# A kernel driven by one list of steps: the list is replaced by another order of the same steps

## The chip, the cores and the metric

The kernel runs on one core of one Trainium2 chip. The metric is the device time of one execution in microseconds, the median of several runs. Before the change it is 539.5 us, from 538.19 to 539.94 in three runs.

## The reference

The inputs are q, k and v of 4 batches, 8 heads, 576 positions and 64 channels, a random matrix omega (128 x 64), and the weights of two layers of experts. Everything is float32.

1. Attention with random features. For each head, phi(x) = exp(x omega^T - |x|^2/2 - max) / sqrt(128), with the maximum over the 128 features of one position. num = phi(q) (phi(k)^T v), den = phi(q) sum(phi(k)), and the output is num / (den + 1e-6).
2. The heads are laid side by side: 2304 tokens of 512 channels.
3. First layer of experts. Each of 8 experts has w1 (512 x 1024) and w2 (1024 x 512). A token goes to the expert with the largest logit; its output is relu(x w1) w2, times the softmax probability of that expert, times a sigmoid gate of that expert.
4. Second layer of experts: the same without the sigmoid gate.

## The kernel before, in words

**Tiling.** Attention works on 16 pairs of heads (4 batches x 4 pairs; the pair's number is one hexadecimal digit). Positions lie in two halves of 288 for q and in chunks of 128 (parts 0: three chunks, 1: two) for k. The expert layers work on 8 units, each one batch in one layer, in the order of `ORDER`; of each unit only the expert that most of its tokens chose is computed for all 576 tokens, weighted by a row of coefficients (zero for other tokens). What is left over is done for up to 8 tokens of one expert by a `Block`, and after that by a loop that seldom runs. Weights and activations of the expert matmuls are split into a high part (`wh`, `xh`, `hh`) and a remainder (`wl`, `xl`, `hl`), and each product is the sum of three matmuls (`TERMS`).

**What sets the order.** The program is emitted under `manual_schedule`: each engine (TensorE, VectorE, ScalarE, GpSimd, and SyncE, whose queue issues nearly all DMAs) executes its instructions in the order of emission, and waits by semaphores for the data and the buffers. The order is the string `PLAN`. A loop at the end of the kernel goes through its words. A number n stands for n expert steps. One expert step is 6 matmuls (line 92); the 512 steps are numbered 0 to 511 here, 64 for a unit, and 32 of these are the first product (every second one ends with an eviction on ScalarE, line 513, and one on VectorE, line 514) and 32 the second (every fourth one ends with an eviction, lines 533 and 535). Expert sums use two PSUM banks, all else the other six. A plus sign behind a copy puts it on VectorE in place of ScalarE.

**The words**, p being the pair:
- `a`, `b`, `c` load q, k and v of a pair (lines 148, 156, 164); `q`, `r` project a half of q and copy it out of PSUM; `t` is the maximum over partitions, an all-reduce on GpSimd (line 226), `s` its subtraction on VectorE (line 230), `x` the exponential on ScalarE. `k`, `m`, `e` project a part of k, take its maximum on VectorE and exponentiate on ScalarE (e: pair, part, head).
- `v`, `w` form phi(k)^T v and copy it; `n`, `d`, `f`, `g` form the numerator, divide, transpose and copy out; `h`, `l` make the high and low parts of the output, `o` stores it.
- `Gu` is the next of 11 stages of unit u's router, numbered G0.0 to G0.10: logits on TensorE, copy, transpose (.2), maximum and mask on VectorE (.3), counting matmul (.4), the expert's number (.5), coefficients (.6, .7), transpose (.8), copy, store. `Pu` reads the expert's number into SyncE; `Wu` loads the coefficients.
- `Fui`, `Hui`, `Lui` fetch tile i of unit u's weights (lines 458 and 463; two staging buffers), make its high part and its remainder (line 486). `Xuc`, `Yuc` (line 552) split the unit's output for the next layer, `Suc` stores it.
- `A` (34 stages) is the block of leftover tokens, `B` (12 stages) adds its result to rows already stored: four loads of old rows (line 757), then additions (line 766) and stores (line 768). `C` and `M` scale and merge. `J` loads the router's weights, `z` are spins of TensorE, `I` and `T` set up.

Of the kernel before, what the change touches and what calls it, by code (L numbers as in the profile page):

```python
# [63 lines left out]
Y02 G2 2 o7 t91 H17 X03+ L17 1 s90 P2 2 x90 4 F20 H20+ m80 ba o5 e801 e800 1 L20 3 Y03 F21 H21 F22 2 s91 6 ab 1 ac H22
2 L21 2 x91 G2 v80 v81 k90 k91 w8+ n80 n81 m90 e900 m91 d80 d81 e901 e910 e911 F23 1 L22 2 ca X10 1 qa0 ka0 ma0 ka1
ra01 ra00 qa1 ra11+ ta1 ma1 1 ea00 G2 1 ea11 1 G2 G2 ra10+ H23+ L23 bb F24 sa1 ea01 1 ta0 v90 v91 sa0 ea10 va0 w9 va1
wa+ S130 xa1 H24+ bc kb0 kb1 kc0 cb xa0 bd mb0 eb01 mb1 eb10 mc0 eb00 3 eb11 G3 n90 G3 ec01 d90 ec00 F25 n91 d91 vb0
vb1 wb+ qb0 rb00 qb1 kd0 rb10+ rb01 kd1 rb11+ kc1 md1 mc1 ed11 ec11 md0 1 L24 1 G3 2 ec10 1 H25+ 3 G3 1 Y10 3 L25 G2
# [5 lines left out]
1 L40 S310 1 h9+ G4 G4 H41 L41 1 F42 F43 l9 1 ha gc0 la hb 2 lb 1 H42 L42 F44 3 H43 L43 ce 8 H44+ 1 F45 1 S330 14 L44
3 F46 2 G4 fc1 gc1+ H45+ qd0 ke0 me0 qd1 rd11 rd10+ rd00+ td0 W4 S320 3 H46 rd01 1 L45 sd0 F47 td1 1 ee01 xd0 3 sd1 1
ee00 qe0 re01 re00+ qe1 kf0 re11 re10 te1 te0 oc xd1 hc+ lc kf1 ke1 me1 ee11 cf mf1 ee10 ef10 1 mf0 se1 xe1 2 ef00 1
S210 se0 ef11 1 o9 nd0 ef01 nd1 dd0 dd1 qf0 rf01 rf00 qf1 rf10 rf11+ 1 tf1 fd0 tf0 gd0 3 fd1 L46 gd1+ xe0 ve0 ve1 sf1
X40 S400 sf0 we xf1 xf0 vf0 ne0 de0 vf1 S300 ne1 wf de1 nf0 hd nf1 df0 df1 ld 1 fe0 fe1 1 H47+ ff0 ff1 ge0 ge1 he+ le
gf0 1 gf1 G5 G5 1 L47 G5 G5 1 G5 1 G5 G5 P5 1 F50 F51 G5 2 S420 2 hf lf 3 H50+ L50 2 G5 H51+ F52 1 S430 L51 1 F53 3
H52 1 Y40 1 G5 G5 2 H53+ 4 of L52 F54 8 L53 F55 9 H54+ L54 1 H55 1 W5 1 G6 X41 2 G6 3 L55 Y41 1 G6 1 X42+ Y42 G6 F56 1  # L80
H56 F57 L56 2 G6 X43 G6 P6 Y43 H57 G6 4 F60 2 L57 od 3 F61 G6 S410 4 H60 L60 H61+ 1 F62 L61 H62 1 L62 4 F63 F64 oe 3
S530 H63+ 4 L63 4 H64 L64 G6 1 F65 2 S500 5 G7 H65 G6 1 G7 G7 G7 L65 1 G7 1 G7 G6 1 F66 1 F67 W6 G7 P7 1 ob G7 T 2 A 1
H66 G7 G7 G7 2 A 2 A S510 S520 2 A 1 W7 A C50 X50 H67 C52 Y50 7 C51 L66 L67 F70 F71 1 C53 A X51 Y51 X52 Y52 3 A 2 X53+
# [891 lines left out]
```

## Time and profile before

| | before |
|---|---|
| median of 3 runs | 539.5 us |
| the profiled execution, whole | 539.03 us |
| its span, first to last instruction | 537.2 us |
| granted TensorE clock, mean | 0.998 |
| DMA | 74.18 MB, 138 GB/s in the mean |

How to read it: times are microseconds from the span's start. An engine's busy time is the union of its instructions. Matmuls overlap in the records (one of 128 x 288 is recorded with some 295 ns, and the next one starts some 133 ns later), so TensorE's pace is read from start to start. A row of the timeline gives start, duration, engine, line, operation, written and read tile, shapes, the count of merged instructions, and in brackets the idle time before it with what ended it. In the names, `qhh<-qhh,qhl` is the subtraction `s`, `PARTITION_ALL_REDUCE qhl<-qhh` the reduce `t`, `wl<-wr,wh` is `L`, `xl<-y,xh` is `Y`, `pc`, `ptc` and `pg` belong to the router, `pm` to the expert steps.

### The profile page before, as it was taken

Reading aid. Unit: us, or ns where it says so; the run is one execution under the profiler, and the core shown is the slowest. Engines: PE = TensorE matmul, PEld = TensorE weight load, DVE = VectorE, ACT = ScalarE, POOL = GpSimd, SP = SyncE. Lnnn points to the kernel's source line nnn. Section 1 sums busy time; section 2 is a strip of 40 time slices with the busy share of each in tenths; the row PEclk is TensorE's granted clock in tenths of the full one; section 3 lists DMA queues with packets and bytes.
Section 4 is the critical chain, followed back from the end, with each engine's and each line's share of the span. In section 5 each row is a group of like instructions: output and inputs, shape, how many; then the busy total and the mean of one; then the engine's idle time right before and its main releaser. Section 6 shows DMA issues by size and latency. Waiting matters only on the chain.

```text
span 537.2 us, 12915 instructions
## 1 busy us (share of the span) xinstructions
PE 525.2 (98%) x5294; PEld 503.6 (94%) x5294; DVE 341.9 (64%) x761; ACT 199.0 (37%) x503; POOL 74.0 (14%) x68
## 2 busy tenths in 40 slices
...
GB/s 307 119 56 218 120 79 177 89 120 88 206 186 153 127 86 149 103 147 177 165 0 106 192 48 98 163 3 195 70 101 146 179 114 140 188 158 89 313 169 182
DMA packets 83954, 74.18 MB, mean 138 GB/s; under 512 B 14256, under 2 KB 68144, under 8 KB 83888
## 3 DMA queue, kind: packets, MB, share of 16 engines
...
q10 hardware_dynamic: 288, 0.13, 0.1%
...
## 4 chain that ended last, share of the span: by engine, by line
PE 88%; DVE 8%; issue 2%; DMA 1%; ACT 1%; POOL 1%; POOLq 0%; DVEq 0%; ACTq 0%
PE pm L92 74%; PE pn L268 3%; PE ph L219 3%; PE ph L185 2%; DVE qhh L230 2%; DVE nm L195 2%; PE pkv L242 2%; PE pg L337 1%; PE pf L302 1%; DVE wl L486 1%; DMA wr<-w1a 1%; PE idle L850 1%; POOL qhl L226 0%; DVE wh L131 0%; DVE xl L320 0%
## 5 line engine op out<-in xcount | busy, mean ns | idle before, releaser
L92 PE MATMUL pm<-xh,wh 128*128 128x288 f32 x512 | 152.8, 298 | 1.1 <-DVE hl L514 1.1
L92 PE MATMUL pm<-hh,wh 128*128 128x288 f32 x512 | 153.4, 300 | 0.0
L92 PE MATMUL pm<-xh,wl 128*128 128x288 f32 x512 | 151.0, 295 | 0.0
L92 PE MATMUL pm<-hh,wl 128*128 128x288 f32 x512 | 150.8, 295 | 0.0
L92 PE MATMUL pm<-hl,wh 128*128 128x288 f32 x512 | 150.8, 294 | 0.0
L92 PE MATMUL pm<-xl,wh 128*128 128x288 f32 x512 | 150.8, 294 | 0.0
L514 DVE SCALAR_TENSOR_TENSOR hl<-pm,hh 128x288 fp32r<-128x288 f32 x128 | 58.3, 456 | 93.7 <-ACT hh L513 93.2
L513 ACT ACTIVATE hh<-pm 128x288 fp32r<-128x288 f32 x128 | 52.8, 412 | 156.3 <-PE pm L92 154.7
L226 POOL PARTITION_ALL_REDUCE qhl<-qhh x32 | 66.8, 2128 | 282.1 <-DVE qhh L131 144.3
L92 PEld LDWEIGHTS pm<-xh,wh 128*128 128x128 f32 x512 | 96.1, 188 | 3.1 <-DVE hl L514 1.5
L92 PEld LDWEIGHTS pm<-hh,wh 128*128 128x128 f32 x512 | 96.2, 188 | 2.5 <-issue 2.0
L92 PEld LDWEIGHTS pm<-hl,wh 128*128 128x128 f32 x512 | 96.1, 188 | 0.0
L92 PEld LDWEIGHTS pm<-xl,wh 128*128 128x128 f32 x512 | 96.1, 188 | 0.0
L92 PEld LDWEIGHTS pm<-xh,wl 128*128 128x128 f32 x512 | 96.1, 188 | 0.0
L92 PEld LDWEIGHTS pm<-hh,wl 128*128 128x128 f32 x512 | 96.0, 188 | 0.0
L486 DVE TENSOR_TENSOR wl<-wr,wh 128x1024 fp32r<-128x1024 f32 (+1 forms) x72 | 81.1, 1139 | 5.9 <-ACT wh L133 5.4
L533 DVE TENSOR_TENSOR y<-pm,cb 128x288 f32<-128x288 f32 x56 | 25.4, 454 | 40.4 <-PE pm L92 36.7
L133 ACT CAST wh<-wr 128x1024 fp32r<-128x1024 f32 (+1 forms) x36 | 35.8, 998 | 40.3 <-DMA wr<-w1b 18.7
L199 ACT ACTIVATE kp<-ph,nm 128x128 f32<-128x128 f32 x140 | 40.2, 382 | 10.1 <-DVE nm L195 10.1
L234 ACT ACTIVATE qhh<-qhh 128x576 f32<-128x576 f32 x32 | 21.9, 697 | 23.1 <-DVE qhh L230 23.0
L230 DVE TENSOR_TENSOR qhh<-qhh,qhl 128x576 f32<-128x576 f32 x32 | 30.0, 944 | 0.4 <-POOL qhl L226 0.3
L195 DVE TENSOR_REDUCE nm<-ph 128x3 f32<-128x384 f32 (+1 forms) x64 | 27.5, 481 | 3.1 <-PE ph L185 2.9
...
## 6 DMA issues: line engine op xcount, KB each, us to landing
...
qr<-qT SPq DMA_DIRECT2D x16, 288.0 KB, 4.4
kr<-kT SPq DMA_DIRECT2D x16, 288.0 KB, 3.9
xd<-xraw SPq DMA_DIRECT2D x16, 288.0 KB, 4.3
```

The lines of the kernel that those rows point to most:

```text
L92: nc.tensor.matmul(out, ws(*t), xs(*t), start=first and t == terms[0], stop=last and t == terms[-1])
L133: nc.scalar.copy(out=out, in_=in_)
L195: nc.vector.tensor_reduce(out=nm[:, j, 0:m], in_=pk, axis=AX.X, op=ALU.max, negate=True)
L199: nc.scalar.activation(self.kp[:, c, j * NF : (j + 1) * NF], self.pk[part][j][:, i * NF : (i + 1) * NF], AF.Exp, bias=self.nm[part][:, j, ...
L219: nc.tensor.matmul(ps[i], om[r, :], self.qr[r, tokens(s)], start=True, stop=True)
L226: nc.gpsimd.partition_all_reduce(qm, qe, 128, bass_isa.ReduceOp.max)
L230: nc.vector.tensor_tensor(out=qe, in0=qe, in1=qm, op=ALU.subtract)
L234: nc.scalar.activation(qe, qe, AF.Exp, scale=SCALE)
L486: nc.vector.tensor_tensor(out=wl[:, p], in0=self.raw[i][:, p], in1=wh[:, p].bitcast(F32), op=ALU.subtract)
L513: nc.scalar.activation(hh[:, s], pm, AF.Relu)
L514: nc.vector.scalar_tensor_tensor(out=hl[:, s], in0=pm, scalar=0.0, in1=hh[:, s].bitcast(F32), op0=ALU.max, op1=ALU.subtract)
L533: nc.vector.tensor_tensor(out=y[:, t], in0=pm, in1=self.cb[:, t], op=ALU.mult)
```

## The change

The string `PLAN` is replaced. Both lists hold the same steps and 512 expert steps; spins are 16 and 11 in place of 16, 8 and 3. Plus signs are 84 in place of 73 (r 13 for 17, g 15 for 8, h 10 for 8, w 6 for 5, X 8 for 5, H 32 for 30). No other line changes. Cut to the parts that matter: the opening up to the first expert steps, the passage from unit 0 to unit 1, the router of unit 3, and the end.

```diff
-a0 I z16 q00 r000+ r001 q01 b0 k00 a1 k01 r010 r011 m00 e000 b1 q10 a2 a3 r101+ z8 q11 t00 r100+ m01 c0 s00 e001 k10
-e011 b2 t01 e010 r110+ k11 b3 v00 v01 c1 c2 c3 x00 m10 r111 t11 t10 a4 s01 e100 x01 m11 w0+ q20 n00 e110 n01 r200+
-e101 q21 r201 s11 a5 e111 k20 r210 d00 d01 r211 k21 x11 v10 m20 v11 e200 s10 w1 b4 f00 b5 f01 t20 m21 g00+ g01+ x10 z3
-n10 e211 t21 q30 s20 e201 q31 e210 s21 h0+ r300 r301 r310 r311 t31 d10 k30 q40 t30 x20 x21 r401 r400 m30 n11 e301 v20
...
-x40 r501 a6 r500 d31 n40 n41 h2 e501 q51 J f30 d40 f31 r510 d41 l2 t50 g30 k51 k60 m51 r511 g31 G0 h3 b7 e510 k61 e511
-G0 G0 m60 e601 c6 e600 s50 a7 v50 m61 e610 G0 t51 G0 e611 b8 l3 f40 g40 v51 o0 k70 w5 k71 G0 x50 s51 m70 m71 q60 x51
-r600 n50 e700 n51 e710 e711 c7 v60 v61 G0 e701 v70 v71 d50 q61 r601 f41 d51 r610 P0 F00 H00+ F01 L00 f50 w7+ f51 1
...
-h6+ l6 q80 h7+ q81 a9 r800 r801 l7 r811 t81 G1 r810+ G1 1 G1 G1 1 G1 G1 t80 G1 1 b9 s80 4 s81 1 G1 x80 2 q90 q91 r901
-r900+ P1 r911 r910 x81 k80 k81 F10 H10+ F11 H11 L10 L11 F12 Y00 G2 X01 m81 1 G2 1 t90 3 F13 1 H12 3 G1 L12 F14 5 G1 G1
...
-o8 qc0 qc1 cc rc00 rc11 cd h8 l8 bf 1 rc01 H32+ L32 F34 1 ae tc1 sc1 1 rc10 2 S220 G3 1 S200 tc0 2 G3 fa0 1 ga0+ 5 fa1
...
-1 S600 1 L74 F76 2 A A 2 A A A A A 5 H75 4 H76+ 1 L75 L76 4 F77 1 A A A 5 A A H77+ 1 A A A L77 A A 3 A 8 A A B B B B B
-M700 B B B M710 S710 B B B M720 B S700 1 S720 4
+a0 I z16 q00 q01 r000+ r001+ b0 k00 k01 r011+ r010 t00 t01 m00 a1 q10 m01 a2 r101 r100+ z11 q11 s00 e001 e011 r111+
+t11 b1 a3 e010 k10 k11 e000 m10 x00 c0 v00 v01 c1 c2 c3 r110 t10 b2 s01 b3 m11 e100 q20 w0+ x01 n00 e101 n01 r200+ s11
+e110 r201 q21 e111 k20 d00 r210 t20 d01 k21 f00 m20 r211 t21 a4 x11 e200 s10 x10 v10 v11 m21 w1+ f01 g00+ e210 e201
+g01 n10 o0 s20 q30 e211 q31 s21 r300 r301 r311 t31 r310 t30 q40 h0+ k30 x20 d10 c4 r401 n11 r400 v20 v21 k31 b4 b5 m30
+e301 d11 e300 x21 q41 w2+ r410 r411 t41 t40 l0 k40 a5 f10 f11 m31 e310 e311 g10 s31 g11 m40 e400 e401 n20 n21 s30 k41
...
+e500 q50 q51 x40 r500 n40 d31 n41 h2 l2 e501 r510 t50 r501 r511 t51 d40 f30 f31 k51 g30 g31 h3 d41 b6 m51 e510 e511
+k60 J m60 G0 k61 G0 e601 G0 b7 b8 s50 x50 m61 e610 e611 e600 v50 G0 l3 G0 v51 k70 c7 w5 f40 G0 g40 s51 k71 P0 F00 F01
+v60 m70 v61 c8 m71 x51 n50 b9 e700 n51 e710 e701 e711 q60 v70 v71 r600 G0 d50 q61 d51 f50 H00+ L00 r601 w7 H01 f41
+g41+ r610+ t60 L01 f51 3 G0 2 F02 F03 2 H02 H03+ 2 L02 2 o2 1 F04 3 L03 2 H04 1 L04 4 a7 2 G0 g50+ 2 r611 t61 2 s61 1
...
+P1 l7 1 F10 5 s80 H10+ L10 s81 q90 r900 r901 q91 r910 k80 F11 r911 t91 t90 H11 L11 k81 ba F12 F13 G2 1 m81 G2 1 G1 1
+Y00 2 H12+ 2 H13+ 2 L12 1 L13 G1 X01 G1 6 F14 H14+ F15 4 H15 3 L14 F16 1 G2 G2 6 G2 S000 L15 W1 1 S030 1 m80 2 Y01 2
...
+1 ed01 2 F30 X13 ed11 g80+ H27 H30 2 Y13 L27 F31 g90 g91+ sb0 G3 5 xb0 1 f81 L30 F32 g81+ H31 na0 na1 da0 da1 nb0 nb1
+qc0 rc00 qc1 rc11 rc10 tc0 G3 1 G3 L31 db0 fa0 2 db1 F33 2 sc0 rc01 tc1 H32+ 2 fa1 kc1 1 mc1 sc1 xc1 1 L32 4 fb0 ga0+
...
+A L76 8 L77 A S610 3 A A A A B B B B B M710 M700 S710 B B B S700 B B B M720 1 B S720 4
```

## Rows read from the trace of the kernel before

**Rows 1.** The page, busy time of each engine and its share of the span.
```profile
PE 525.2 (98%) x5294; PEld 503.6 (94%) x5294; DVE 341.9 (64%) x761; ACT 199.0 (37%) x503; POOL 74.0 (14%) x68
```
**Rows 2.** The chain of waits: start, duration, instruction, count of merged ones.
```profile
54.81 24.00 PE pm L92 x180
...
445.66 64.43 PE pm L92 x486
```
**Rows 3.** Busy time by stretch: length, then each engine's time (instructions), clock, DMA.
```profile
20.00:40.00 20.00, 19.28 (x376) 16.08 (x373) 18.76 (x46) 18.89 (x61) 9.06 (x6) 1.00 0.29 84
```
**Rows 4.** TensorE's waits: who waited for whom, total, times, longest.
```profile
PE pby L734 <- ACT yc L728: 0.4, 1, 0.4
```
**Rows 5.** Timeline of VectorE and GpSimd, 11.9 to 15 us.
```profile
11.98 1.67 DVE L230 TENSOR_TENSOR qhh<-qhh,qhl 128x576 f32<-128x576 f32 x1
14.80 0.80 DVE L230 TENSOR_TENSOR qhh<-qhh,qhl 128x576 f32<-128x576 f32 x1
...
11.89 1.96 POOL L226 PARTITION_ALL_REDUCE qhl<-qhh  x1 [0.93 <-ACT qhh L133]
13.76 2.04 POOL L226 PARTITION_ALL_REDUCE qhl<-qhh  x1
```
**Rows 6.** Timeline of VectorE, GpSimd and TensorE, 42 to 45.5 us.
```profile
42.44 1.71 DVE L230 TENSOR_TENSOR qhh<-qhh,qhl 128x576 f32<-128x576 f32 x1
...
42.31 2.04 POOL L226 PARTITION_ALL_REDUCE qhl<-qhh  x1
...
45.25 0.20 PE L378 MATMUL pc<-top,unit 72*128 72x64 bf16 x1 [1.09 <-DVE top L364]
```
**Rows 7.** The same three engines, 113 to 122 us.
```profile
113.97 0.46 DVE L533 TENSOR_TENSOR y<-pm,cb 128x288 f32<-128x288 f32 x1 [0.59 <-PE pm L92]
115.69 3.37 DVE L486 TENSOR_TENSOR wl<-wr,wh 128x512 fp32r<-128x512 f32 x3
118.98 1.69 DVE L552 TENSOR_TENSOR xl<-y,xh 128x576 fp32r<-128x576 f32 x1
...
118.10 2.78 POOL L226 PARTITION_ALL_REDUCE qhl<-qhh  x1
...
121.76 0.40 PE L92 MATMUL pm<-xh,wh 128*128 128x288 f32 x1 [1.05 <-DVE hl L514]
```
**Rows 8.** The same three engines, 241 to 245.5 us.
```profile
242.00 1.70 DVE L230 TENSOR_TENSOR qhh<-qhh,qhl 128x576 f32<-128x576 f32 x1
...
241.47 2.43 POOL L226 PARTITION_ALL_REDUCE qhl<-qhh  x1
...
245.03 0.22 PE L427 MATMUL ptc<-ident,g 72*64 72x72 f32 x1 [1.05 <-DVE g L423]
```
**Rows 9.** Timeline of SyncE's issues, ScalarE and VectorE, 48 to 58 us.
```profile
48.06 1.01 SPq L458 DMA_DIRECT2D wr<-w1a  x2
...
54.26 1.05 ACT L133 CAST wh<-wr 128x1024 fp32r<-128x1024 f32 x1 [0.45 <-DMA wr<-w1a]
...
55.34 2.02 DVE L486 TENSOR_TENSOR wl<-wr,wh 128x1024 fp32r<-128x1024 f32 x1 [0.40 <-ACT wh L133]
57.28 0.45 DVE L514 SCALAR_TENSOR_TENSOR hl<-pm,hh 128x288 fp32r<-128x288 f32 x1
```
**Rows 10.** SyncE's issues, TensorE, VectorE, 17 to 30 us; the page's DMA issues.
```profile
17.08 0.92 SPq L156 DMA_DIRECT2D kr<-kT  x2
...
26.44 1.15 PE L185 MATMUL ph<-omk,kr 64*128 64x128 f32 x12
...
28.81 1.01 DVE L195 TENSOR_REDUCE nm<-ph 128x3 f32<-128x384 f32 x2
...
kr<-kT SPq DMA_DIRECT2D x16, 288.0 KB, 3.9
```
**Rows 11.** The page's DMA issues (last: median us to landing); VectorE at 522 us.
```profile
outT<-y SPq DMA_DIRECT2D x15, 288.0 KB, 4.9
...
522.28 0.82 DVE L766 SCALAR_TENSOR_TENSOR old<-by,state,old 128x576 f32<-128x576 f32 x1 [2.14 <-POOL by L745]
```

More of the change, by code (lines that the diff above doesn't have):

```diff
@@ L54 @@
-s30 d20 k50 x31 t40 m41 x30 t41 e411 d21 f20 f21 s41 m50 e410 v40 v41 h1 w3 s40 n30 x41 e500 n31 w4 l1 g20 g21 q50 d30
-x40 r501 a6 r500 d31 n40 n41 h2 e501 q51 J f30 d40 f31 r510 d41 l2 t50 g30 k51 k60 m51 r511 g31 G0 h3 b7 e510 k61 e511
-G0 G0 m60 e601 c6 e600 s50 a7 v50 m61 e610 G0 t51 G0 e611 b8 l3 f40 g40 v51 o0 k70 w5 k71 G0 x50 s51 m70 m71 q60 x51
-r600 n50 e700 n51 e710 e711 c7 v60 v61 G0 e701 v70 v71 d50 q61 r601 f41 d51 r610 P0 F00 H00+ F01 L00 f50 w7+ f51 1
-g41+ r611+ H01 L01 2 t61 F02 1 H02 1 L02 F03 1 H03+ 4 F04 1 G0 1 H04 L03 6 L04 h4+ 2 w6 3 s61 7 G0 G0 F05 g50 g51 H05+
@@ L64 @@
[L64 to L68, printed above, removed]
@@ L69 @@
-o4 6 F26 F27 be 1 tb0 2 S100 sb0 xb0 W2 H26+ X11 Y11 S110 6 X12 G3 H27+ f80 1 S120 Y12 X13 1 L26 ad tb1 f90 G3 g90
-ed10 2 P3 ed00 7 Y13 1 sb1 L27 F30 F31 H30+ L30 xb1 2 g80 1 ed01 2 f81 G3 g81 H31 na0 F32 da0 na1 nb0 da1 nb1 L31 F33
-o8 qc0 qc1 cc rc00 rc11 cd h8 l8 bf 1 rc01 H32+ L32 F34 1 ae tc1 sc1 1 rc10 2 S220 G3 1 S200 tc0 2 G3 fa0 1 ga0+ 5 fa1
-db0 db1 2 G3 H33 G3 W3 L33 1 H34+ ga1 fb0 oa fb1 f91 g91 gb0 gb1+ 2 sc0 1 xc1 xc0 G4 G4 L34 vc0 vc1 vd0 wc nc0 nc1 dc0
-dc1 vd1 3 S230 1 wd 19 af 2 F35 H35+ L35 F36 4 G4 F37 G4 2 G4 H36+ fc0 H37 1 L36 1 G4 3 L37 P4 2 G4 G4 4 F40 F41 1 H40
@@ L74 @@
[L74 to L83, printed above, removed]
@@ new lines @@
+e110 r201 q21 e111 k20 d00 r210 t20 d01 k21 f00 m20 r211 t21 a4 x11 e200 s10 x10 v10 v11 m21 w1+ f01 g00+ e210 e201
+g01 n10 o0 s20 q30 e211 q31 s21 r300 r301 r311 t31 r310 t30 q40 h0+ k30 x20 d10 c4 r401 n11 r400 v20 v21 k31 b4 b5 m30
+e301 d11 e300 x21 q41 w2+ r410 r411 t41 t40 l0 k40 a5 f10 f11 m31 e310 e311 g10 s31 g11 m40 e400 e401 n20 n21 s30 k41
+d20 v30 m41 v31 c5 k50 x31 e411 e410 d21 a6 w3 s41 f20 f21 h1 x30 m50 l1 g20 g21 v40 s40 v41 c6 x41 w4 n30 d30 n31
+e500 q50 q51 x40 r500 n40 d31 n41 h2 l2 e501 r510 t50 r501 r511 t51 d40 f30 f31 k51 g30 g31 h3 d41 b6 m51 e510 e511
@@ new lines @@
+qa0 ra00 F23 F24 ab S130 ra01 H23+ ka0 ma0 G2 ea00 ka1 bc ma1 qa1 ra10 ra11 ta1 ta0 2 ea01 1 ea11 L23 ea10 1 G2 G2 H24
+L24 G2 ac v90 va0 va1 v91 w9 wa kb0 kc0 kb1 mb0 eb00 sa1 eb01 o4 mb1 sa0 cb eb11 2 eb10 1 G3 G3 n90 mc0 ec00 n91 vb0
+Y10 vb1 ec01 bd qb0 wb d90 kd0 d91 S120 kd1 rb00 md1 rb01 S100 cc md0 qb1 rb11 tb1 rb10 tb0 1 G3 f80 2 ed10 sb1 6 W2 8
+cd 2 F25 H25 F26 o5 H26 2 o7 1 be 4 xa0 f90 ed00 G3 X11+ 2 G3 f91 L25 1 S200 xa1 L26 F27 G3 1 P3 1 xb1 2 Y11 X12+ Y12
+1 ed01 2 F30 X13 ed11 g80+ H27 H30 2 Y13 L27 F31 g90 g91+ sb0 G3 5 xb0 1 f81 L30 F32 g81+ H31 na0 na1 da0 da1 nb0 nb1
@@ new lines @@
+qc0 rc00 qc1 rc11 rc10 tc0 G3 1 G3 L31 db0 fa0 2 db1 F33 2 sc0 rc01 tc1 H32+ 2 fa1 kc1 1 mc1 sc1 xc1 1 L32 4 fb0 ga0+
+ga1+ 1 H33+ 2 ec10 ec11 ad gb0+ 1 fb1 gb1 3 G4 L33 vc0 bf G4 vd0 F34 G3 vc1 vd1 wc+ h8+ xc0 H34 L34 ob nc0 nc1 dc0 F35
+5 G3 W3 H35+ 4 L35 3 l8 S220 5 F36 1 H36 L36 3 G4 G4 F37 3 dc1 1 H37+ L37 G4 G4 2 P4 1 S230 4 F40 1 H40 1 F41 2 h9+ 7
+H41 G4 1 S310 2 L40 L41 1 F42 wd 4 l9 ha la hb lb H42+ 4 L42 1 F43 H43 1 L43 F44 F45 3 G4 4 G4 2 ae G4 af H44+ 3 H45+
+2 S330 1 L44 3 G4 F46 L45 1 W4 3 H46 3 fc0 ke0 qd0 gc0+ qd1 F47 rd10 L46 me0 1 rd00 td0 rd01 rd11 td1 S320 1 o9 1 H47
@@ new lines @@
+sd0 xd0 L47 ee00 4 sd1 2 ee01 qe0 re01+ re00 qe1 re10+ te0 re11 te1 S210 oa kf0 ke1 me1 kf1 mf1 mf0 ef10 ee11 ee10
+ef11 xd1 2 X40+ se1 2 ef01 1 fc1 gc1+ nd0 se0 oc ef00 xe0 hc+ xe1 nd1 qf0 dd0 qf1 lc rf10+ rf01 rf11 tf1 dd1 rf00 tf0
+ce 4 fd0 fd1 ve0 cf ve1 gd0 sf1 gd1+ xf1 we+ sf0 vf0 od xf0 ne0 vf1 de0 wf ne1 de1 nf0 df0 nf1 df1 1 fe0 ge0 fe1 S410
+1 ge1+ ff0 gf0 ff1 1 gf1 S300 hd+ ld he+ le G5 G5 hf+ 1 G5 lf G5 1 G5 2 G5 P5 1 G5 G5 F50 1 F51 5 G5 G5 G5 1 H50+ L50
+1 H51+ 4 L51 1 Y40 4 F52 H52+ 2 X41 1 F53 2 L52 3 F54 2 H53 1 oe 1 L53 F55 1 H54 7 W5 2 S400 L54 S420 2 G6 G6 H55+ 1
```

16 lines of the change are left out of this document (11 added, 5 removed).

## The prediction

> **What bounds the kernel now.** I read the page first. TensorE is busy for 98% of the span [rows 1], so nothing but TensorE's own waits and the opening can give time back. The chain of waits says where it is full: from 445.66 us on, 486 block matmuls follow one another in 64.43 us, 132.6 ns each [rows 2]; no order of steps makes that shorter, and both lists hold the same matmuls. The first long run of them begins at 54.81 us [rows 2]. Ahead of it stands the attention of batch 0, and there the windows show VectorE as full as TensorE (18.76 of 20 us between 20 and 40) [rows 3]. TensorE's waits of a microsecond are three after the first spin: pc in the opening [rows 6], pm at 121.76 [rows 7] and ptc at 245.03 [rows 8]. The 0.4 of pby [rows 4] is part of a matmul, copy, transpose sequence that is adjacent in both lists, so it stays.
>
> All three have one cause, which the timelines show when VectorE is laid beside GpSimd. A VectorE instruction with its operands in SBUF that starts shortly behind the start of a GpSimd all-reduce takes about 0.95 us longer. In the opening, subtraction s01 starts 0.09 us behind its reduce and takes 1.67 us; s11 starts 1.04 behind the next one and takes 0.80 [rows 5]. s50 starts 0.13 behind a reduce and takes 1.71, and pc then waits for VectorE until 45.25 [rows 6]. Y00 (0.88 behind, 1.69 us) precedes the eviction that pm waits for [rows 7]; sc1 (0.53 behind, 1.70) precedes the gate step that ptc waits for [rows 8]. I call this a collision: 0.95 us of VectorE for a start within about 1 us of a reduce's start, nothing later than that.
>
> The Trainium skill's page "SBUF — State Buffer" (section "Who interferes with whom") says that whichever of the two starts first keeps the shared ports for the whole instruction and the other blocks fully. By that, s11 could not have ended before 15.80, where its reduce ends; the trace has it end at 15.60. The measurement decides here. By the page's rule the new list's s50 would be held until its reduce ends, some 0.8 us more than I reckon below, and the sum would be 538.2.
>
> **The change part by part.** The sum is made against the profiled execution: span 537.2, 539.03 in all (1.83 around the span). The median of the runs is 539.5, so what comes out below is taken off 539.5.
>
> Opening. The steps ahead of the first expert step are nearly the same set, and TensorE's are exactly the same, 27 spins included. Two things differ in time. First, pair 1's copies: the new list has r111+ on VectorE right behind s00, in place of r111 on ScalarE behind an exponential. The reduce t11 waits for that copy. It started at 11.89 [rows 5]; r111+ would end at about 11.0 (s00's end by the trace, 10.7, plus a copy of 0.36 from start to start), so t11 starts at 11.05, and s01, which cannot start before 11.95, is 0.9 behind it instead of 0.09. It keeps 0.1 of its 0.95: s01 and what follows come 0.8 earlier. VectorE then waits for k20 at about 17, so I let 0.6 of it through. Second, q51 and r510 stand ahead of n40 in place of behind f30: t50 starts at 39.2 instead of 39.83, its successor t51 ends its first microsecond at 42.2, and s50, at about 42.4, goes free: 0.9 off the chain s50, m61, top, pc, and as much off the expert's number, which the first weight load waits for. Against that VectorE has more to do: w1+ and w2+ (about 0.2 each), six copies r of batch 0 for five (0.36), and g01 leaves it (0.28): 0.5 later. Sum of the opening: -0.6 - 0.9 + 0.5 = -1.0. Its bounds: 0, if what is late next is weight tile 1. It is issued right behind the two halves of tile 0; ScalarE's copy of it starts on its landing at 54.26, L01 ends at 57.36, and the eviction of step 1 stands behind that until 57.73, when step 4 wants its bank [rows 9]. These move with the expert's number, by 0.9 at most, and L01 has a collision of its own (2.02 us) that the new list keeps. At the other end -1.5, if both gains arrive in full.
>
> Unit 1's first matmuls (pm, 1.05). Between the last eviction of unit 0 (step 63, from 113.97 to about 114.35) and the one that step 68 waits for, the old VectorE order is r900+, H10+, L10, L11, Y00, m81; the new one s80, H10+, L10, s81, L11, m81, with Y00 behind the eviction. Two subtractions (0.74 each) in place of a copy and Y00 (0.36 + 0.67) are 0.45 more, but VectorE need not wait for q90's matmul (0.8). Added up from 114.35: s80 115.1, H10 115.8, L10 117.0, s81 117.75, L11 118.9, m81 119.55, eviction 120.0, where step 68 is due at 120.5. The slack is 0.5 and the two reduces t91 and t90 still fall into this stretch: no collision costs nothing, one 0.45, two 1.4. L10 and Y00 had one each (the 3.37 us of three L instructions hold the first, rows 7). I take 0.6, near to one: a gain of 0.45, bounds -0.35 and 1.05.
>
> Unit 2's gate (ptc, 1.05). The new list puts G3.7 behind da1 and ahead of step 183, and no reduce starts there before it: L30 1.24, g81+ 0.28, da0 0.83, da1 0.67, G3.7 0.79 make 3.8 us of VectorE against f, n and q matmuls and one step, 4.7 us of TensorE. It has 0.9 to spare, so the 1.05 goes. Bounds 0 and 1.05.
>
> What is new and could cost. Eleven more copies go to VectorE in all (84 plus signs for 73), 5.1 us of VectorE and 6.5 fewer of ScalarE; beside some 480 us of expert steps, with VectorE busy for 64% of the span [rows 1], that is hidden except where VectorE stands in a burst. I allow 0.4 for one half collision at a tight place (the gate and kp steps with under 0.4 to spare); bounds 0 and 1.5.
>
> What I cost at nothing. (a) SP's queue: o0, the store of pair 0's output, now stands ahead of c4, b4, b5, a5 and c5, and waits for g01, at about 21. b4 was issued with b5 at 17.08 and now goes at about 22. A load of this kind lands 3.9 us later; k40 ran at 26.44 and m40, its reader, started at 28.81 [rows 10]. VectorE's order covers it; without that cover, in the slowest case (c5, behind it in the same burst, took 5.6), k40 is late by 1.2 and m40 by nothing. (b) J, the gates' weights, now waits behind c6 for v41 (35.4) and is issued at about 36 instead of 31.3; landing after 3.7 us it precedes G0.0 at 41.25 by 1.5. (c) c8, b9 and a7 now stand behind F00 and F01; their readers are units later. (d) In the tail S610 now stands right ahead of the loads of old rows. If these wait until it has landed (4.9), old arrives by about 522 instead of 518, and the block's first addition starts at 522.28 behind GpSimd in any case [rows 11]; the last eviction, ten microseconds later, does not see it.
>
> Sum: -1.0 - 0.45 - 1.05 + 0.4 = -2.1. 539.5 - 2.1 = 537.4 us.
>
> **The rivals.**
> - The opening's gain is eaten by weight tile 1 and the eviction behind L01, and t91 and t90 collide twice: 0 - 1.05 + 0.35 + 0.4 = -0.3, 539.2. For it: L01's collision stays, and two reduces remain at the tight place. Against it: tile 1's issue moves with the expert's number.
> - Slower: new collisions in the stretch from 14 to 38 us, where VectorE goes from one instruction to the next and hands every delay on to the first expert step. The old list has five from s01 [rows 5] to s50 [rows 6], s01, l0, s31, s30 and s50, of 0.35 to 1.1 us. The new order of reduces (t31, t30, t41, t40) meets l0, s31, s30, s41 and s40 at other moments. Each one more costs 0.95; two more cancel the forecast's gain, and from four on the kernel is slower than can be taken for no change: 4 x 0.95 - 2.1 = +1.7, 541.2. For it: nothing in either list keeps these starts apart. Against it: of the old five, two go by the reckoning above, so that six new ones would have to come.
> - More than forecast: the opening gives 1.5, pm goes altogether, nothing new is met: -1.5 - 1.05 - 1.05 = -3.6, 535.9.
>
> **How the numbers follow.** A measurement of this kernel can tell about 0.3%, 1.6 us, from no change. Forecast (537.4; its own range 536.4 to 538.3) 0.38, first rival 0.35, slower 0.15, more 0.12. The range for 8 in 10 goes from 535.7 to 540.4. Faster, below 537.9: 0.12 and nearly all of the forecast, 0.48. Within: 0.37. Slower: 0.15.
>
> **What would show it.** Right: s01 near 0.75 us long; s50 too, with pc waiting for VectorE less than 0.4; the first long run of block matmuls at about 53.8; no ptc wait; a pm wait at step 68 of 0 to 1.4. Wrong: b4's landing behind 27.6 with m40 waiting for k40; a first expert step later than 54.8; more than five subtractions of batch 0 of over 1.05 us; a wait for weights (hl, wl) in a later unit, which no row of before shows.

## The result and the profile after

The changed kernel takes 534.22 us (median of 5 runs, 533.15 to 534.61); beside them the kernel before took 539.94 (538.19 to 541.34). The ratio is 0.9896, 95% interval [0.9867, 0.9925]: 5.6 us, 1.0% faster, where 2.1 us were forecast. Its profiled execution took 534.12, with a span of 532.3.

The page's first part and the end of the chain of waits, of the kernel after (answering [rows 1, 2]). TensorE is busy as long as before, and 4.4 of the 4.9 us that the span lost were its idle time. The experts start at 51.52, 3.0 earlier, but their first long run only at 55.45: a wait at step 4 cuts it in two. The chain in front of that wait is the landing of weight tile 1 (52.72), L01, and the eviction of step 1 behind it.

```profile
PE 524.7 (99%) x5294; PEld 503.8 (95%) x5294; DVE 341.7 (64%) x771; ACT 190.8 (36%) x493; POOL 71.7 (13%) x68
```

```profile
46.51 6.18 DMA wr<-w1a
52.72 1.06 ACT wh L133
53.84 1.11 issue
54.94 0.46 DVE hl L514
55.45 0.66 PE pm L92 x3
...
441.68 63.64 PE pm L92 x480
```

TensorE's waits of the whole kernel after: who waited for whom, total, times, longest. The 1.1 us of pc, of pm at step 68 and of ptc ([rows 6 to 8]) are gone; pby [rows 4] is there, and one pm wait is new, the one of 0.5 at step 4 in the chain above.

```profile
PE idle L850 <- POOL zeros L828: 1.1, 1, 1.1
PE pm L92 <- DVE hl L514: 0.5, 1, 0.5
PE ph L219 <- DMA qr<-qT: 0.5, 1, 0.5
PE pby L734 <- ACT yc L728: 0.4, 1, 0.4
PE pn L268 <- ACT kp L199: 0.3, 1, 0.3
```

The same view of the kernel before, from 10 to 56 us alone. Of these the prediction names only the first; the sum is 3.5 us, and after has 0.3 ahead of its first expert step in that stretch.

```profile
PE pc L378 <- DVE top L364: 1.1, 1, 1.1
PE pn L268 <- DVE kvr L131: 0.7, 1, 0.7
PE pkv L242 <- ACT kp L199: 0.5, 1, 0.5
PE pn L268 <- ACT qhh L133: 0.5, 1, 0.5
PE pf L302 <- DVE kvr L131: 0.3, 1, 0.3
PE ph L185 <- DVE qhh L131: 0.2, 1, 0.2
PE pf L302 <- ACT kp L199: 0.2, 1, 0.2
```

A subtraction that a reduce does not touch takes 0.75 us; one that takes longer is called held here. VectorE's timeline after, and GpSimd's below it: s01 and s50 (answering [rows 5, 6]), s31 and s30 between them, L10 and s81 ahead of step 68 [rows 7]. s01 starts 0.94 us behind its reduce, s50 1.01 behind t51 (the second half of the 3.91). Neither takes more than 0.83. In a second trace of the changed kernel s50 takes 0.83 again, but s01 starts 0.68 behind its reduce and takes 1.07.

```profile
11.68 0.82 DVE L230 TENSOR_TENSOR qhh<-qhh,qhl 128x576 f32<-128x576 f32 x1
...
26.45 0.75 DVE L230 TENSOR_TENSOR qhh<-qhh,qhl 128x576 f32<-128x576 f32 x1
28.05 0.77 DVE L230 TENSOR_TENSOR qhh<-qhh,qhl 128x576 f32<-128x576 f32 x1
...
40.50 0.83 DVE L230 TENSOR_TENSOR qhh<-qhh,qhl 128x576 f32<-128x576 f32 x1
...
113.30 2.23 DVE L486 TENSOR_TENSOR wl<-wr,wh 128x512 fp32r<-128x512 f32 x2
115.46 0.74 DVE L230 TENSOR_TENSOR qhh<-qhh,qhl 128x576 f32<-128x576 f32 x1
```

```profile
10.74 3.91 POOL L226 PARTITION_ALL_REDUCE qhl<-qhh  x2 [0.66 <-DVE qhh L131]
...
37.62 3.91 POOL L226 PARTITION_ALL_REDUCE qhl<-qhh  x2 [6.66 <-DVE rd L289]
...
113.72 2.09 POOL L226 PARTITION_ALL_REDUCE qhl<-qhh  x1 [7.24 <-ACT qhh L133]
```

Expert steps of all the traces, laid side by side. "Start" is the first key matmul of pair 1 (k10; 9.64 us before), which moves by up to 1 us with the first loads. The next columns are the starts of expert steps 0, 8, 72, 216 and 511 against the kernel before, each counted from k10. "End" is the time from VectorE's last instruction to the end of the span (4.16 before). The new opening does three more spins ahead of k10 and three fewer behind it; they take TensorE 0.4 us before (19.75 to 20.18), so its rows show up to 0.4 us of gain that only this way of counting makes.

```
trace               k10    step 0     8     72    216    511    end
after              +0.24   -3.28  -2.51  -3.58  -5.25  -5.00   4.00
after, again       -0.06   -2.85  -2.39  -3.37  -5.04  -4.97   4.45
new open, old rest -0.20   -2.89  -1.84  -1.85  -1.85  -1.86   5.63
  the same, again  -0.30   -2.86  -1.75  -1.75  -1.72  -1.73   5.89
old open, new rest +0.21   +0.36  +0.29  -0.73  -2.40  -2.36   4.02
old, fills         -0.15   -0.30  -0.31  -1.59  -3.09  -3.19   4.40
new, fills         +0.34   -1.55  -1.28  -2.54  -4.09  -2.82   5.33
Y00, sc1 moved     +0.11   -0.03  -0.03  -1.35  -2.55  -2.50   4.39
r111 for r110      -0.71   -0.97  -0.98  -0.97  -0.98  -0.94   3.28
  the same, again  -1.00   -1.01  -1.01  -1.01  -0.99  -0.99   5.87
pair 5's order     -0.34   -0.85  -0.86  -0.86  -0.85  -0.85   3.38
four moves         -0.30   -0.30  -0.32  -1.62  -2.80  -2.81   4.39
new, r110 back     +0.31   -1.51  -1.04  -2.10  -3.77  -3.35   4.00
l0 behind s31      -0.34   +0.03  +0.03  +0.03  +0.02  +0.02   4.38
m31 ahead of l0    -0.35   +1.35  +1.34  +1.35  +1.35  +1.36   5.92
five (l0)          +0.45   -1.17  -1.17  -2.47  -3.68  -3.64   5.52
five (m31)         -0.04   -1.15  -1.16  -2.47  -3.68  -3.69   3.34
new, L01 and A.28  +0.38   -2.88  -2.94  -2.68  -4.35  -4.63   6.11
new, A.28 alone    -0.55   -2.89  -2.03  -3.09  -4.58  -4.95   5.57
```

Of the 5.0 us at the last step, 2.5 stand at step 8 (the opening) and 1.05 more at step 72 (pm). The rest is not ptc alone. Between steps 72 and 216 the two lists also place the steps differently among TensorE's other work; taken where the same work is done, both traces of after gain 0.8 at step 136 and 0.8 more by step 203 (ptc), and lose 0.1 to 0.3 again by step 303. The place at step 136 is one that neither the prediction nor an experiment names. Before, L23 starts 0.45 us behind a reduce and takes 2.05; the copy `w` that follows it is late, and a weight load of TensorE waits 0.34 for it, which the view of the matmuls' waits does not list. After, L23 is free:

```profile
183.53 2.05 DVE L486 TENSOR_TENSOR wl<-wr,wh 128x1024 fp32r<-128x1024 f32 x1
183.08 2.23 POOL L226 PARTITION_ALL_REDUCE qhl<-qhh  x1 [0.62 <-DVE qhh L131]
187.53 0.63 PEld L185 LDWEIGHTS ph<-omk,kr 64*128 64x128 f32 x9 [0.34 <-DVE kvr L131]
...
181.70 1.23 DVE L486 TENSOR_TENSOR wl<-wr,wh 128x1024 fp32r<-128x1024 f32 x1 [0.54 <-PE pkv L242]
```

The end is as long as before.

### The profile page after: what moved, and what is told of

The parts are those of the page before. It is cut to its first block, busy times and chain, and to the rows that moved or that the text cites. A ratio compares the mean times of both kernels' runs of the same rounds, so it can differ in the third digit from the quotient of the medians.

```text
span 532.3 us, 12918 instructions
## 1 busy us (share of the span) xinstructions
PE 524.7 (99%) x5294; PEld 503.8 (95%) x5294; DVE 341.7 (64%) x771; ACT 190.8 (36%) x493; POOL 71.7 (13%) x68
## 4 chain that ended last, share of the span: by engine, by line
PE 94%; DMA 2%; DVE 1%; ACT 1%; issue 0%; SPq 0%
PE pm L92 77%; PE pn L268 4%; PE ph L219 3%; PE ph L185 3%; PE pkv L242 3%; PE pg L337 2%; PE pf L302 1%; DMA wr<-w1a 1%; DMA qr<-qT 1%; DVE nm L195 1%; PE pyc L726 0%; PE pu L705 0%; PE pt L346 0%; PE idle L850 0%; ACT wh L133 0%
## 5 line engine op out<-in xcount | busy, mean ns | idle before, releaser
L226 POOL PARTITION_ALL_REDUCE qhl<-qhh x32 | 65.1, 2075 | 278.7 <-ACT qhh L133 245.2
L486 DVE TENSOR_TENSOR wl<-wr,wh 128x1024 fp32r<-128x1024 f32 (+1 forms) x72 | 79.8, 1122 | 12.0 <-ACT wh L133 11.0
L133 ACT CAST wh<-wr 128x1024 fp32r<-128x1024 f32 (+1 forms) x35 | 34.0, 973 | 45.2 <-DMA wr<-w1b 22.8
L230 DVE TENSOR_TENSOR qhh<-qhh,qhl 128x576 f32<-128x576 f32 x32 | 27.6, 865 | 1.3 <-POOL qhl L226 1.3
```

The lines of the kernel that those rows point to most:

```text
L133: nc.scalar.copy(out=out, in_=in_)
L226: nc.gpsimd.partition_all_reduce(qm, qe, 128, bass_isa.ReduceOp.max)
L230: nc.vector.tensor_tensor(out=qe, in0=qe, in1=qm, op=ALU.subtract)
L486: nc.vector.tensor_tensor(out=wl[:, p], in0=self.raw[i][:, p], in1=wh[:, p].bitcast(F32), op=ALU.subtract)
```

## The experiments

My theory: a VectorE instruction is held by a reduce that has just started, TensorE pays where that instruction stands right ahead of what it reads, and these few places make the whole gain. The rivals: the gain is spread over the burst (VectorE has less to do ahead of a deadline), or it comes from the eleven copies that went to VectorE.

**Each half alone.** The new list's steps up to the first expert steps with the old list's rest, and the other way round.

```diff
-PLAN = old list
+PLAN = new list up to step 0 of unit 0, then the old list    # new open, old rest
+PLAN = old list up to there, then the new list               # old open, new rest
```

> The new list up to the first expert step, the old list behind it (steps that the new opening already holds are left out there, a7 is put at its start). In the trace of after, step 4 begins 2.37 us earlier than before, so if the opening's gain is handed on: 539.9 - 2.4 = 537.5 us, with the old waits of 1.05 at pm (step 68) and at ptc (G3.8) still in it. Rival, the two parts hang together (the old rest meets the earlier opening with new waits): 539 or more.

> The old list up to the first expert step, the new list behind it (c8, b9, H01, g41+, t60 and L01 are put at its start, a7 is left out there). By the traces the rest gains 4.76 - 2.37 = 2.4 us: 537.5, without waits at step 68 and G3.8. Rival, the new rest needs the new opening: 539 or more.

Old opening, new rest: 537.28 us, ratio 0.9964 [0.9949, 0.9978]; both 1.05 waits are gone. New opening, old rest: 539.06, ratio 0.9999 [0.9988, 1.001], although every expert step is 1.8 us earlier. A second trace of it:

> The new list's opening with the old rest a second time, for another trace. In the first the expert steps were 2.05 us earlier from step 8 to the last, and the span was 0.6 shorter. If the order alone sets it, the steps stand as in the first trace to within 0.3 us, counted from the first key matmul; what is lost then stands behind the last matmul (last store issued or landed 1 to 2 us later than in the kernel before) or ahead of the first.

It took 538.66 in its one run. The steps are the first trace's to within 0.13 us, and the end is 5.89 us long instead of 4.16. So in these two traces the steps are the same, and the end can take 1.5 us or more back.

**No reduce at all.** In both lists GpSimd copies 8 columns and fills the rest with zeros instead of reducing; the maximum over partitions is left out.

```diff
-            nc.gpsimd.partition_all_reduce(qm, qe, 128, bass_isa.ReduceOp.max)
+            nc.gpsimd.tensor_copy(out=qm[:, 284:292], in_=qe[:, 284:292])
+            for n in (S, S, S, HS):
+                nc.gpsimd.memset(qm[:, 0:n], 0.0)
```

> The old list, with each all-reduce on GpSimd replaced by an instruction sequence that lasts about as long, 2.0 us (a copy of 8 columns that reads both halves of q, then four fills of the result with zeros), so that nothing waits for less but GpSimd hardly reads SBUF; the maximum over partitions is left out of the computation. Theory of collisions (a VectorE instruction on SBUF that starts within 1 us of a reduce loses up to 0.95): the six of the opening lost 4.2 us of VectorE between them, the three behind it 2.2 of TensorE; without them the opening ends 2 to 3 us earlier and the waits at step 68 and G3.8 go: 534.5 to 536. Rival, the order itself (what stands behind what on each engine) makes the difference of the two lists: 539 to 540, no change.

> The same replacement in the new list; the maximum over partitions is left out. Theory of collisions: the new list has one in the opening and none that TensorE waits for, so it gains 0 to 0.8 us: 533.4 to 534.2, and the two lists with fills lie within 1.5 us of each other, where they are 5.7 apart with reduces. Rival, the order itself: the distance of 5 us stays.

Old list 535.44, ratio 0.9930 [0.9911, 0.9948]; new list 536.36, ratio 0.9947 [0.9934, 0.9960]. VectorE's 32 subtractions, by line and form, of the old list with fills:

```profile
L231 DVE TENSOR_TENSOR qhh<-qhh,qhl 128x576 f32<-128x576 f32 x32 | 24.1, 753 | 7.0 <-POOL qhl L227 6.9
```

753 ns in the mean, against 944 in the kernel before and 865 after: a fill holds nobody, the reduce does. The old list loses its pm wait, all but 0.2 of its ptc wait, and 0.65 at steps 135 and 136, where L23 now takes 1.23. But copy and fills take 2.5 us or more (3.4 at most in the old list), longer than the reduce, and VectorE now waits 6.9 us for them in all. The old list's opening is 1.57 us ahead at q61, the last projection of pair 6 (41.42 us behind k10, 42.99 before); then VectorE waits 0.35 and 0.73 for the two halves of weight tile 0, and 0.3 is left at step 0. The new list missed its forecast of 533.4 to 534.2: it is slower than with the reduces. So the run shows the cause of the holds; it does not price the opening.

**The two places behind the opening**, in the old list:

```diff
-F12 Y00 G2 X01 m81 1 G2 1 t90 3
+F12 G2 X01 m81 1 G2 1 Y00 t90 3
-ae tc1 sc1 1 rc10 2 S220 G3 1
+ae tc1 1 rc10 2 S220 G3 sc1 1
```

> The old list with two steps moved by a few places: Y00 from ahead of m81 to behind it (beside step 68), and subtraction sc1 from ahead of gate step G3.7 to behind it. Theory A (a late reader at one tight place each): TensorE's two waits of 1.05 us, for the eviction at step 68 and for ptc, both go, nothing takes their place, the expert steps are 1.05 earlier from step 72 and 2.1 earlier from step 200 on: 539.0 - 2.1 = 536.9 us (536.2 to 537.6). Theory B (the burst as a whole is too long for VectorE, and what is moved is only late elsewhere): a wait of 0.5 to 1 us shows a few steps later at each place, and the time is 538.2 or more.

536.39 us, ratio 0.9941 [0.9924, 0.9958]. TensorE's waits in it hold neither pm nor ptc any more, and nothing replaces them (the smaller lines, as before, left out):

```profile
PE idle L849 <- POOL zeros L827: 1.1, 1, 1.1
PE pc L377 <- DVE top L363: 1.1, 1, 1.1
PE pn L267 <- DVE kvr L130: 0.7, 1, 0.7
```

Theory A holds: two steps moved by a few places are worth 2.5 us at the last step, about what the new list's rest gains (2.65 from step 8 to the last with the old opening). The theory had 2.1, since it took the waits as the view gives them. A wait of 1.05 costs 1.2, because the record of the matmul ahead of it reaches 0.29 us from its start while the pace is 0.13: before step 68, matmuls start at 120.41 and 121.76.

**The places in the opening**, one at a time in the old list:

```diff
-e010 r110+ k11 ... x00 m10 r111 t11
+e010 r111+ k11 ... x00 m10 r110 t11            # r111 for r110
-x40 r501 a6 r500 d31 n40 n41 h2 e501 q51 J f30 d40 f31 r510 d41 l2 t50 g30 k51 k60 m51 r511 g31
+x40 r500 a6 q51 n40 d31 n41 h2 l2 e501 r510 t50 r501 r511 J f30 d40 f31 d41 g30 k51 k60 m51 g31
```

> The old list with one pair of copies exchanged: r111 of pair 1 on VectorE in the place of r110, and r110 on ScalarE where r111 stood; no other step moves. Theory A (a subtraction that starts with a reduce takes 0.95 us longer, and that is handed on): reduce t11 starts at about 11.1, s01 is 0.75 to 0.85 us long, n00 starts 0.8 to 1.1 us earlier, and at step 0 of the experts 0.6 to 1.0 is left; 538.0 to 538.5 us. Theory B (the opening of the new list gains because more copies run on VectorE and ScalarE's chain is shorter): the number of copies on each engine is as before, so step 0 moves by less than 0.3 and the time is 539.0. Theory C (everything behind it in the opening meets the reduces at other moments): s01 is free, yet other subtractions (l0, s31, s30) change by up to 1 us each, and step 0 moves by anything between -2 and +1.

> The old list with pair 5's steps in the new list's order: q51 ahead of n40, r500 ahead of r501, r510 and reduce t50 behind e501, r501, r511 and t51 ahead of f30. Theory A (collision of s50 with reduce t51): t51 starts at about 41 in place of 42.31, s50 is about 0.8 us long in place of 1.71, TensorE's wait of 1.09 for pc is under 0.4, and the first expert step is 0.7 to 1.0 earlier; by step 8 some of it may be given back at the eviction behind L01: 538.1 to 538.8 us. Theory B (the gain of the opening stands in the number of copies that VectorE takes): step 0 moves by less than 0.3, 539.0.

Pair 5's order: 537.80 us, ratio 0.9969 [0.9953, 0.9986]; s50 takes 0.87 and every step is 0.85 earlier. That is theory A. r111 for r110: 539.52, ratio 1.0007 [0.9994, 1.0020], and yet every step is 0.97 earlier from k10 on. s01 there:

```profile
11.26 1.00 DVE L229 TENSOR_TENSOR qhh<-qhh,qhl 128x576 f32<-128x576 f32 x1
```

It starts 0.76 behind its reduce (10.50) and ends 1.76 behind it. l0, s31 and s30 are held as in the kernel before (1.81, 1.38, 1.09), and the exchange adds no copy to VectorE, so B is out. Theory C is not: l2 and s50 have changed places. Before, l2 starts 0.01 us behind t50 and is free, and t50 and t51 take 4.52 together in place of 3.91; with r111, l2 starts 0.02 behind t50 and is held, and s50 goes free. Before, then with r111:

```profile
39.84 0.75 DVE L320 TENSOR_TENSOR xl<-xraw,xh 128x576 fp32r<-128x576 f32 x1
39.83 4.52 POOL L226 PARTITION_ALL_REDUCE qhl<-qhh  x2 [8.79 <-ACT qhh L133]
...
38.46 1.74 DVE L319 TENSOR_TENSOR xl<-xraw,xh 128x576 fp32r<-128x576 f32 x1
41.72 0.74 DVE L229 TENSOR_TENSOR qhh<-qhh,qhl 128x576 f32<-128x576 f32 x1
38.44 3.91 POOL L225 PARTITION_ALL_REDUCE qhl<-qhh  x2 [8.79 <-ACT qhh L132]
```

TensorE's wait for pc falls to 0.49 by that. So s01's own price is the 0.68 by which n00 is earlier (4.25 us behind k10, 4.93 before); the other 0.3 is s50's. For the gain that the median lacks, a second trace:

> The old list with r111 for r110 a second time, for another trace: the first profiled execution (span 534.6) was the fastest of twelve, whose median lay 2.9 us higher. Theory A (the order of steps alone sets the time): the expert steps start as in the first trace to within 0.1 us once both are laid together at the first key matmul, and only the start differs. Theory B (transfers land at other moments in each execution, and this opening has less in hand against them): TensorE or VectorE waits 0.5 to 2 us for a load (x, k, v, q or a weight tile) between 20 and 60 us, which the first trace does not show. Theory C (the end): the last store starts or lands 1 to 2 us later behind the last matmul.

538.76 in its one run. The steps again stand 1.0 earlier; the end is 5.87 us, against 3.28 in the first trace, which was the fastest of twelve. That is theory C, the end, as far as one trace can say.

**All four together.**

> The old list with all of it: r111 for r110, pair 5's order, Y00 and sc1 moved. Theory A (four places, each with its own wait, that add up): step 0 is 1.5 to 2 earlier, step 72 on 2.5 to 3, step 200 on 3.6 to 4.1: 535.0 to 535.5 us, most of what the new list gains (539.0 x 0.9896 = 533.4). Theory B (the gains don't add, since the weight of tile 1 and the eviction behind L01 hold the experts back): step 8 is not over 1 us earlier, and the time is 536.5 or more. Theory C (the gain of the new list is spread over its many other moves): under a third of the 5.6 us, 537.2 or more.

534.84 us, ratio 0.9918 [0.9900, 0.9937], 4.1 us of the new list's 5.6, with the same number of copies on VectorE as before; so those 4.1 need none of the eleven. Places add up: in the trace q61 is 1.53 earlier, 0.68 of s01 and 0.87 of pair 5, and the two places behind the opening give 2.5 again. But the profiled execution was one of the slower two of six (536.15), and the four show only 2.81 us at the last step, because VectorE waited for the second half of weight tile 0 in between:

```profile
50.33 0.42 DVE L130 CAST wh<-wr 128x512 fp32r<-128x512 f32 x1
51.88 0.43 DVE L130 CAST wh<-wr 128x512 fp32r<-128x512 f32 x1 [1.13 <-DMA wr<-w1a]
```

**The exchange undone in the new list.**

```diff
-e011 r111+ t11 b1 ... c3 r110 t10
+e011 r110+ b1 ... c3 r111 t11 t10
```

> The new list with that one exchange undone: r110 on VectorE, r111 on ScalarE behind x00, reduces t11 and t10 behind it. Theory A (only s01's hold of 0.85 us comes back): t11 starts at about 11.9, s01 is 1.7 us long, step 0 of the experts 0.6 to 0.9 later, 534.8 us or about 0.6 above the changed kernel. Theory B (the whole opening stands otherwise to the reduces): l0, s31 or s30 are held too (1.0 us or more long), step 0 is 1.2 to 2 later, 535.5 to 536. Theory C (worth nothing, VectorE's wait for k20 takes it up): within 0.3 us of the changed kernel.

> The changed kernel unaltered, beside the three others on one chip: 0.9896 of the kernel before, about 533.5 us; the two kernels above are compared with it.

535.98 us, ratio 0.9931 [0.9917, 0.9945], against 534.53, 0.9911 [0.9895, 0.9927] for the changed kernel beside it: 1.45 us dearer. s01 is free (0.75), but s11 takes 1.71 and s10 1.41. So theory B, in other subtractions than I had named.

**l0, s31 and s30.** Two tries to free them in the old list, each alone and with the four moves:

```diff
-d11 l0 e300 m31 r410 k40 f10 s31 r411
+d11 e300 m31 r410 k40 f10 s31 l0 r411          # l0 behind s31
+d11 e300 m31 l0 r410 k40 f10 s31 r411          # m31 ahead of l0
```

> The old list with one step moved: l0, the low half of the gate's input of pair 0, from behind d11 to behind subtraction s31. In the kernel before l0 starts 0.03 us behind a reduce and takes 1.81 us, s31 0.38 behind the next (1.38), s30 0.75 behind the third (1.09). Theory A (a held instruction ends 1.84 us behind the reduce's start, and the delay is handed on): with l0 later, s31 is at most 0.95 long, l0 and s30 are free, VectorE is 1.2 to 1.8 us earlier at s30, TensorE's idle 0.52 us at v30 and 0.18 at f20 go, and the experts start 0.5 to 0.7 us earlier, counted from the first key matmul: 538.5 us. Theory B (the time between 25 and 31 us is TensorE's own): the holds go, the experts start less than 0.2 earlier, 539.1.

> The old list with l0 and m31 exchanged: m31, which reads PSUM, stands where the reduce starts, and l0 behind it. Worked out with the rule that a held instruction of VectorE ends 1.84 us behind the start of the reduce (0.03 less for l0's other length): m31 25.2 to 25.9, l0 held by 0.2 to 26.9, s31 26.9 to 27.6 ahead of the next reduce (27.13) and free, m40 27.6 to 28.7, s30 28.7 to 29.45 ahead of the third (28.99) and free, all counted from the first key matmul of the kernel before. Theory A: TensorE's idle 0.52 us at v30 and 0.18 at f20 go, and the experts start 0.5 to 0.7 earlier, counted from the first key matmul. Theory B (the hold moves to another instruction again, as it did in the first try): one of l0, s31, m40, s30 is held by 0.5 or more, less than 0.3 arrives at v30. The time itself may move by as much as the end's own scatter of 1.5 us.

> The old list with the four moves (r111, pair 5's order, Y00, sc1) and l0 behind s31. Theory A (places add up): 0.5 to 0.7 us under the four moves, 534.2 us, level with the changed kernel (534.2 and 534.5 so far). Theory B (what is late next is the landing of the first weight tiles, which is issued with the expert's number and takes 4 to 5 us): the opening's further gain stops at VectorE's wait for these tiles, and the time stays at 534.8.

> The old list with five places mended: r111, pair 5's order, Y00, sc1, and l0 behind m31. Theory A (places add up): TensorE's steps up to q61 0.5 to 0.7 earlier than with the four, counted from the first key matmul, and the time 534.2, level with the changed kernel. Theory B (the landing of weight tile 0, issued with the expert's number, is late next): q61 is earlier and VectorE then waits 0.5 to 1.6 us for the tile; the time stays at 534.8.

All four missed: 540.07 (ratio 1.0014 [0.9999, 1.0028]), 539.55 (1.0002 [0.9986, 1.0019]), 535.26 (0.9925 [0.9910, 0.9940]) and 535.55 (0.9922 [0.9905, 0.9938]). The hold goes to whichever subtraction then meets a reduce. With five places TensorE's wait at v30 is 1.0 us in place of 0.5, and VectorE waits for no weight tile, so theory B's reason is not what the traces show either. VectorE's timeline with l0 behind s31, where the next reduce starts at about 26.8:

```profile
26.52 0.75 DVE L229 TENSOR_TENSOR qhh<-qhh,qhl 128x576 f32<-128x576 f32 x1
27.19 1.70 DVE L319 TENSOR_TENSOR xl<-xraw,xh 128x576 fp32r<-128x576 f32 x1
28.81 1.01 DVE L194 TENSOR_REDUCE nm<-ph 128x3 f32<-128x384 f32 x2
29.75 1.09 DVE L229 TENSOR_TENSOR qhh<-qhh,qhl 128x576 f32<-128x576 f32 x1
```

With m31 ahead, m31 has to wait for k31's matmuls (until 26.12, counted as before), which I had overlooked; then s31 takes 1.70. That execution also shows that one list does not always meet the reduces in the same way. Up to d11 its steps are those of the kernel before, but s00 and s01 are free and s11 and s10 are held:

```profile
9.23 0.84 DVE L229 TENSOR_TENSOR qhh<-qhh,qhl 128x576 f32<-128x576 f32 x1
11.30 0.74 DVE L229 TENSOR_TENSOR qhh<-qhh,qhl 128x576 f32<-128x576 f32 x1
13.90 1.71 DVE L229 TENSOR_TENSOR qhh<-qhh,qhl 128x576 f32<-128x576 f32 x1 [0.20 <-POOL qhl L225]
18.08 1.42 DVE L229 TENSOR_TENSOR qhh<-qhh,qhl 128x576 f32<-128x576 f32 x1
```

**Two tries to beat the changed kernel**, on the two waits that it has left:

```diff
-t60 L01 f51 3 G0 2 F02
+t60 f51 2 L01 2 G0 1 F02                       # new, L01 and A.28
-1 A A A L76 8 L77
+1 A A L76 1 A 7 L77                            # in both
```

> The new list with two steps moved: weight subtraction L01 from ahead of the eviction of step 1 to behind it, and the gate step G0.7 behind step 3; and one expert step between the two steps of the last stage (A.27, A.28) whose matmul waits for a copy. Theory A (the rule of the late reader): the changed kernel's wait of 0.51 us at step 4 and its wait of 0.4 for pby go, the time is 0.5 to 0.9 us below the changed kernel's on the same chip, about 533.0. Theory B (L01 is then late for step 8, which reads tile 1): a wait of 0.3 to 1 us for the weights appears instead, and nothing is gained.

> The new list with one thing moved: an expert step between the two steps of the last stage (A.27 and A.28) whose transpose waits for a copy of ScalarE. TensorE's wait of 0.39 us goes: 0.4 us under the changed kernel, 534.0 on this chip, if the end stays as long; a rival is that nothing is gained, because the last stores wait for SP's branch and what is loaded behind it.

With both 536.60, ratio 0.9939 [0.9923, 0.9955]: the wait at step 4 goes, but VectorE then waits for weight tile 2, an eviction queued behind that copy is late, and TensorE pays 1.07 at 61.32. VectorE's timeline there:

```profile
60.20 0.69 DVE L131 CAST wh<-wr 128x1024 fp32r<-128x1024 f32 x1 [2.14 <-DMA wr<-w1a]
60.81 0.45 DVE L514 SCALAR_TENSOR_TENSOR hl<-pm,hh 128x288 fp32r<-128x288 f32 x1
```

With A.28 alone 534.86, ratio 0.9923 [0.9905, 0.9940]: the pby wait is gone, the end was 5.57 us long in that trace, and the time is level with the changed kernel. Nothing tried is faster than it.

## Why the prediction was wrong, step by step

The mechanism was right, and so were the three places that the prediction named. The step that failed is the sum of the opening, put at -1.0 with bounds of 0 and -1.5: it gave 2.4 to 2.5 at step 8 (up to 0.4 of it the three spins). It left TensorE's four waits of 0.2 to 0.5 at nothing and took 0.5 off for copies that cost nothing. Behind the opening it put pm at -0.45, where 1.05 came, and had nothing for step 136, which gave 0.8.

- **s01: -0.6.** Right in kind: s01 is 0.82 long (1.07 in the second trace). About right in size: r111 alone makes n00 0.68 earlier, which is TensorE's wait there (pn for kvr, 0.7). The reason was another: VectorE's wait for k20 was to take part of 0.8, but what TensorE had waited is all that it could win. In the changed kernel n00 stands 1.1 us earlier.
- **s50: -0.9.** Right: 0.83 long, pc's wait from 1.09 to under 0.2, and pair 5's order alone gives 0.85.
- **VectorE's additional work: +0.5.** Wrong: nothing of it shows. Ahead of step 0 TensorE waits longer than before in two places alone, for the first q load (0.5) and at n10 (0.3).
- **Not reckoned at all:** waits of 0.5 and 0.2 (v30 and f20, behind the held l0, s31 and s30), and of 0.5 and 0.3 (n50, and pf just ahead of step 0). In the changed kernel l0, s31 and s30 take 0.75, 0.75 and 0.77, and v30 stands 0.6 us better than n20. I had these three among the dangers of the slower rival, and never asked what it is worth if the new order misses them. That they caused the 0.7 is read from the traces side by side; no experiment freed them, since both tries only moved the hold (and with one more of it ahead of v30, the wait there grew to 1.0).
- **The cap.** The first rival's reason was right and its size was wrong. The chain above ends the opening with weight tile 1, which lands at 52.72, L01 and the eviction behind it: 0.7 of 3.3 us is given back at step 4 (0.4 in the second trace). I had let these move by 0.9 at most; the issue moved by 2.8, from [rows 9]'s 48.06 to 45.24, since the whole opening moved. The landing of tile 1 moved by only 1.5, because it came 6.2 us behind its issue in place of 4.9. Nor did the new list keep L01's hold: L01 takes 1.23 (1.55 in the second trace) in place of 2.02.
- **pm at step 68: -0.45, bounds up to -1.05.** 1.05 came. One hold of 0.95 fell into the stretch (the second half of L10, 1.63 us of the 2.23 for two), as I had put it, but it cost only 0.13: the slack was not 0.5 us but about 0.8. The eviction ends at 118.37, and without the hold would have ended at 117.42; step 68 starts at 118.42 and was due at 118.29.
- **ptc: -1.05.** Right that the wait goes. With the place moved alone it gave 1.2; in the changed kernel 0.8 are left of it by step 203, and what takes the rest stays open.
- **New costs: +0.4.** No wait of a listed size showed, but the 0.4 just named and the 0.1 to 0.3 lost between steps 203 and 303 are about this much. SyncE's queue, J and the loads moved behind others show no cost, as said: no expert step waits 0.2 us or more for weights after tile 1.
- **The slower rival.** Its four new holds did not come: of the opening's subtractions none is longer than 0.83 but s00 (1.45), and in the second trace s00 and s01 (1.56 and 1.07).
- **The Trainium skill's rule.** The Trainium skill's "SBUF — State Buffer", section "SBUF: two separate sides", says of an instruction with two SBUF inputs and a GpSimd instruction that reads SBUF that the first keeps the shared ports for its whole length. By that, s50 would have stayed until its reduce ends, at 41.53; it ended at 41.33, and the sum by that rule, 538.2, is farther off than mine.

So the terms would have been -0.7 -0.2 (s01 and TensorE's 0.2 ahead of it), -0.9 (pc), -0.7 and -0.8 (the four small waits), +0.8 given back (0.5 at step 4, 0.3 at n10): -2.5, then -1.05 and -1.05: 4.6, and 534.9 from 539.5. All but the 0.8 given back were lines in the profile of before. That this comes so near to 534.2 is partly luck: it has neither step 136, nor the spins, nor what was lost again behind step 136.

Open: why kernels that differ from the old list only in the opening (r111, both l0 tries, new opening with the old rest) show no better median than before although all but the l0 tries have earlier steps, while pair 5's order alone does (537.80). Their traces put the loss into the end, but one or two traces stand for twelve runs. The other runs may also have met the reduces otherwise, as the m31 trace did; nothing here tells the two apart.
